# Sixteen pieces of like length: a recurrent chain dealt out anew between attention steps

## Chip, core and metric

The kernel runs on one core of a Trainium2 chip. The metric is the device time of one launch in microseconds, taken as the median of the runs.

## What is computed

One training step of a gated mix of two sequence layers on 2,048 tokens of width 576, with all gradients. Cut to the forward pass:

```
g   = sigmoid((x * gate_w).sum(-1))
a   = A(x)      # attention, 32 heads of 18; one k and one v head for all of them
b   = B(x)      # 64 segments of 32 tokens, 32 heads of 128, one after the other:
      h   = [mem (8 rows), segment (32 rows)]
      q, k, v = h Wq, h Wk, h Wv                 # masked softmax attention in h
      o   = softmax(q k^T * scale + mask) v Wo
      mem = o[:8]; the segment's output is o[8:]
out = g * a + (1 - g) * b
```

The outputs are `out` and the gradients of a scalar product with `grad_out`, for the input and every weight. Inputs and outputs are bf16.

## The kernel before

**Stages.** The program is a row of stages. First come weights and transposes, and projections of the tokens. Then comes the stage that the change is about, the forward weave. After it come all of layer B's token rows in bulk, a second weave (the chain backward with pass 2 of attention A), and the weight gradients.

**The weave.** `weave` takes two Python generators and alternates between them: one piece of the chain, then one step of the sweep, with the order of instructions on each engine just as written (`manual_schedule`). The chain is `b_chain_fwd`: layer B's eight memory rows through 64 segments, 16 pieces to a segment. The sweep is `a_pass1`: 1,024 steps, 16 for each block of one head pair and 512 queries. So piece i of a segment always stands before step i of a block.

**A step.** Step n issues on PE the scores matmuls `a_S` of step n+1 (two tiles of 32 rows), the matmuls `a_dP` of step n, the products with `a_W` of step n-1, and the products with `a_E` of step n, both into `a_acc`. ACT takes the exp of the scores (line 1401, 128x1024), DVE multiplies `a_dP` by `a_E` into `a_W` (line 1434, two instructions). `a_S` has one buffer of two PSUM banks, `a_dP` three of one bank, `a_acc` one. At the end of a block, in its step 16, ACT copies `a_acc` into `a_acs` (line 1439). The first product of the next block waits for that copy, and it is issued in step 1.

**Post-processing of a block.** `a_post` has three parts, which the sweep calls at the end of steps 1, 4 and 6 of the next block. The first transposes `a_acs` in f32 on PE, and ACT copies the result to `a_tk` (line 1472). The second transposes `a_QD`, and ACT copies it to `a_qt` (line 1478, one buffer). The third is one reciprocal on DVE, eleven small operations on POOL, and three stores on SP: `otok`, `dqtok` (lines 1498, 1504) and `sd` from `a_qt` (line 1508). The parts use the chain's PSUM tile `c_pj`.

**A piece.** The chain's projections are [40 rows of memory and riding tokens] x 576 x 4,096 for each of k, q and v, in two halves j. A half is 20 matmuls: five k-tiles of 128 rows, each with four matmuls of 512 columns on the four column tiles of the array. It accumulates in one PSUM bank, and ACT moves it to SBUF (`evac`, line 63). The pieces of a segment before:

| piece | work on PE |
|---|---|
| 0, 1 | k projection, half 0, half 1 |
| 2 | transpose of k (`mem_T`, 8 matmuls with full-width weights) |
| 3, 4 | q projection |
| 5 | transpose of q |
| 6 | v projection, half 0 |
| 7 | scores of 32 heads, 65 small matmuls (`ps`), then exp |
| 8 | denominator (2 matmuls), then reciprocal on DVE |
| 9 | v projection, half 1 |
| 10 | transpose of v |
| 11 | product with v (`po`, 16 matmuls) |
| 12, 13, 14 | output projection in thirds of 256, 256 and 64 columns (32 matmuls each); sums over head groups of the third before (f32 matmuls) |
| 15 | last sum; DVE copies the new memory into `hm` (line 419) |

The projections, the v transpose and the thirds use the PSUM tile `c_pj`, the others `c_x`; each is one bank with one buffer.

**Riding tokens and transfers.** Beside the memory rows, `hm` carries up to 24 tokens whose q, k and v are wanted later in the chain. SP loads them a segment ahead (line 254). In the first 48 segments SP also transposes the weight heads, two a segment, into the one buffer `c_wt` (line 275), and stores each again (line 279, `stash_end`). SP further copies rows between DRAM buffers (lines 303, 305), loads `c_kx` (line 262), `c_vx` (line 268) and `a_QD` (line 1390), and writes `oh`. Transfers of POOL carry the projected rows out. All of SP's transfers go out in the order written.

Of the kernel before, what the change touches and what calls it, by code (L numbers as in the profile page):

```python
# [10 lines left out]
F32 = mybir.dt.float32  # L11
P = 128

D = 576
NKT = 5
# [15 lines left out]
class Kern:  # L31
# [205 lines left out]
    def b_chain_fwd(self, keep, sp, psum):  # L237
        nc = self.nc
        NSEG = self.NSEG
# [3 lines left out]
        for kt in range(NKT):  # L243
            rows = KT_ROWS[kt]
            nc.gpsimd.dma_start(hm[0][0:rows, kt, 0:8], self.B_mem0[:, kt * P:kt * P + rows].rearrange("m d -> d m"))

        def ride(s):
            t0 = self.XT0 * P + 24 * s
            return t0, max(0, min(24, self.T - t0))

        def load_ride(s):
            t0, n = ride(s)
            if n:
                nc.sync.dma_start(hm[s % 2][:, :, 8:8 + n], self.xT_dram[:, :, t0:t0 + n].rearrange("k p t -> p k t"))
# [23 lines left out]
        def stash_end(t, c):  # L278
            nc.sync.dma_start(self.st_WT[c // HB][:, c % HB, :], t[:])
# [3 lines left out]
        def flat(t, j):  # L283
            return t[:, 4 * j:4 * j + 4, :].rearrange("p u e -> p (u e)")

        kx, vx = load_k(0), load_v(0)
        for s in range(NSEG):
            h_ = hm[s % 2]
            nc.gpsimd.dma_start(self.memT_dram[:, :, s, :], h_[:, :, 0:8])
            t2 = {w: sp.tile([P, 8, E], BF16, name=f"c_{w}2", bufs=1) for w in ("k", "q", "v")}  # L290
            mT = {w: sp.tile([P, 4, 8, 8], BF16, name=f"c_{w}mT", bufs=2) for w in ("k", "v")}

            def head_out():
                c0 = 8 * (s % 16)
                nc.sync.dma_start(self.oh_dram[s // 16][:, :, c0:c0 + 8], oh[:].rearrange("p c u q -> p (c u) q"))

            def rows_out(w):
                nc.gpsimd.dma_start(self.row_dram[w][s], t2[w][:].rearrange("p u e -> p (u e)"))

            def rows_copy(w):  # L300
                src = self.row_dram[w][s].rearrange("(c r) e -> c r e", r=32)
                t0, n = ride(s)
                nc.sync.dma_start(self.mtok[w][s * 8:(s + 1) * 8, :].rearrange("r (c e) -> c r e", c=4), src[:, 0:8, :])
                if n:
                    nc.sync.dma_start(self.xtok[w][t0:t0 + n, :].rearrange("r (c e) -> c r e", c=4), src[:, 8:8 + n, :])

            def mT_out(w, src):
                nc.scalar.copy(mT[w][:].rearrange("p c u t -> p u c t"), src)
                nc.gpsimd.dma_start(self.mTd[w][s], mT[w][:].rearrange("p c u t -> p (c u) t"))

            def proj(w, j):
                pj = self.proj_mem(h_, self.W[w], j, psum, "c_pj", 1)
                self.evac(flat(t2[w], j), pj[:], use="s")

            if 0 < s <= 48:
                stash_end(*wt)
            for j in range(2):
                proj("k", j)
                if j == 0:
                    if s + 1 < NSEG:  # L320
                        load_ride(s + 1)
                    nc.gpsimd.dma_start(self.pq_dram[s // 4].rearrange("s q c w k -> (s q c) w k")
                                        [:, 4 * (s % 4):4 * (s % 4) + 4, :], self.zeros[:].unsqueeze(1).to_broadcast([P, 4, P]))
                yield
            src = self.mem_T(t2["k"], psum, "c_x", 1)
            mT_out("k", src)
            rows_out("k")
            yield
            for j in range(2):
                proj("q", j)  # L330
                yield
            src = self.mem_T(t2["q"], psum, "c_x", 1)
            qT = sp.tile([P, 8, 4, 8], BF16, name="c_qT", bufs=1)
            nc.vector.tensor_copy(qT[:], src)
            rows_out("q")
            yield
            rows_copy("k")
            proj("v", 0)
            if s < 48:
                wt = stash(2 * s)  # L340
            yield
            ps = psum.tile([P, P], F32, name="c_x", bufs=1)
            self.mm(ps[:], lhsT=self.identB[:], rhs=self.mbias[:], start=True, stop=False)
            for u in range(8):
                for c in range(4):
# [6 lines left out]
            Et = sp.tile([P, 2, 64], BF16, name="c_E", bufs=1)  # L352
            nc.scalar.activation(Et[:].rearrange("p a b -> p (a b)"), ps[:], ACT.Exp, scale=SCALEB)
            yield
            den = psum.tile([P, 64], F32, name="c_x", bufs=1)
            self.mm(den[:], lhsT=self.blockones[:], rhs=Et[:, 0, :], start=True, stop=False)
            self.mm(den[:], lhsT=self.blockones[:], rhs=Et[:, 1, :], start=False, stop=True)
            rd = sp.tile([P, 64], F32, name="c_rd", bufs=1)
            nc.vector.reciprocal(rd[:], den[:])
            yield  # L360
            proj("v", 1)
            if s + 1 < NSEG:
                kx = load_k(s + 1)
            pn = sp.tile([P, 2, 64], BF16, name="c_pn", bufs=1)
# [4 lines left out]
            rows_out("v")  # L369
            yield  # L370
            rows_copy("q")
            src = self.mem_T(t2["v"], psum, "c_pj", 1)
            mT_out("v", src)
            yield
            po = psum.tile([P, 8, 32], F32, name="c_x", bufs=1)
# [10 lines left out]
            if s + 1 < NSEG:  # L386
                vx = load_v(s + 1)

                def half(lo, hi):
                    ph = psum.tile([P, 512], F32, name="c_pj", bufs=1)  # L390
                    for u in range(8):
                        for g in range(4):
                            self.mm(ph[32 * g:32 * g + 32, 0:hi - lo], lhsT=oT[:, u].rearrange("p c q -> p (c q)"),
                                    rhs=self.WoN[:, 8 * g + u, lo:hi], start=(u == 0), stop=(u == 7), tp=(0, 32 * g))
                    return ph

                def sums(hs, kts):
                    for n, kt in enumerate(kts):
                        ncols = KT_ROWS[kt]
                        self.mm(pm[0:ncols, kt, :], lhsT=hs[:, n * P:n * P + ncols], rhs=self.selF[:, :])  # L400

                head_out()
                rows_copy("v")
                if s < 48:
                    stash_end(*wt)
                    wt = stash(2 * s + 1)
                hn = hm[(s + 1) % 2]
                hs = None
                pm = None
                for lo, hi in ((0, 256), (256, 512), (512, 576), (576, 576)):  # L410
                    if hi > lo:
                        ph = half(lo, hi)
                    if lo:
                        kts = range(lo // P - 2, min(lo // P, NKT)) if lo < 576 else (4,)
                        if pm is None:
                            pm = psum.tile([P, NKT, 8], F32, name="c_x", bufs=1)
                        sums(hs, kts)
                        r = 64 if lo == 576 else P
                        nc.vector.tensor_copy(hn[0:r, kts[0]:kts[-1] + 1, 0:8], pm[0:r, kts[0]:kts[-1] + 1, :])
                    if hi > lo:  # L420
                        hs = sp.tile([P, 256], F32, name="c_hs", bufs=1)
                        nc.scalar.copy(hs[:, 0:hi - lo], ph[:, 0:hi - lo])
                    yield
            else:
                yield
                head_out()
                rows_copy("v")
                yield
# [950 lines left out]
    def a_pass1(self, keep, sp, psum, xps):  # L1379
        nc = self.nc  # L1380
# [34 lines left out]
        post = None  # L1415
        for n in range(NP_ + 1):
            if n < NP_:
                kt = n % 16
                if kt == 8:
                    load(n // 16 + 2)  # L1420
                if n > 1 and n % 16 == 1:
                    acc = psum.tile([P, 512], F32, name="a_acc", bufs=1)
                    acc_mm(acc, n - 1, E_, self.VK, True, False)
                if n + 1 < NP_:
                    mm_S(n + 1)
                dP = [psum.tile([P, 512], F32, name="a_dP", bufs=3) for _ in range(2)]
                for i in range(2):
                    r = slice(64 + 32 * i, 96 + 32 * i)
                    self.mm(dP[i][:], lhsT=self.KV[r, kt * P:kt * P + P], rhs=QD[n // 16][r, :], tp=(64 + 32 * i, 0))
                if n + 1 < NP_:  # L1430
                    ex(n + 1)
                W_[n] = sp.tile([P, 2, 512], BF16, name="a_W", bufs=2)
                for i in range(2):
                    nc.vector.tensor_tensor(out=W_[n][:, i, :], in0=dP[i][:], in1=E_[n][:, i, :], op=ALU.mult)  # L1434
            if n > 0:
                acc_mm(acc, n - 1, W_, self.WK, False, n % 16 == 0)
                if n % 16 == 0:
                    acs = sp.tile([P, 512], F32, name="a_acs", bufs=1)
                    nc.scalar.copy(acs[:], acc[:])
                    bb = n // 16 - 1  # L1440
                    post = self.a_post(bb // 4, bb % 4, acs, QD.pop(bb), sp, xps, dl_all)
            if n < NP_:
                if n == 0:
                    acc = psum.tile([P, 512], F32, name="a_acc", bufs=1)
                if n % 16 or n == 0:
                    acc_mm(acc, n, E_, self.VK, n == 0, False)
            if post is not None and n % 16 in (1, 4, 6):
                if next(post, "end") == "end":
                    post = None
            yield  # L1450
# [359 lines left out]
```

The softmax here doesn't subtract the row's maximum and nothing guards it: scores larger than these inputs give would overflow.

## Time and profile before

| | |
|---|---|
| three runs | 6,305.22, 6,307.33 and 6,308.78 us |
| profiled execution | span 6,318.6 us |
| PE busy in the span | 5,710.0 us, 90% |
| DVE, ACT, POOL busy | 59%, 55%, 31% |
| forward weave (first to last `a_S` matmul) | 507.7 to 2,393.2 us |
| TensorE clock granted, 1,000 to 1,200 us | 1.00 |

The profile records one execution, some 11 us longer than the runs. A matmul's row gives the time until its modelled end; the next one starts earlier, since matmuls are pipelined, so lengths of pieces are read from starts. In a line of the timeline the first number is the start in us, the second the length, then engine, line of code, operation and tiles; the brackets give idle time of the engine and what ended it. SP has rows only for what its queue issues.

### The profile page before, as it was taken

How to read it: one execution, taken by the hardware profiler on the slowest of the kernel's cores; microseconds unless marked ns; L12 is line 12 of the kernel's file. 1: busy time of each engine (PE TensorE's matmuls, PEld its weight loads, DVE VectorE, ACT ScalarE, POOL GpSimd, SP SyncE). 2: the span in 40 equal slices, each digit the busy share in tenths (PEclk: the TensorE clock that was granted, in tenths of full speed). 3: DMA queues.
4: the chain of work that ended last, by engine and by line, in shares of the span. 5: the costliest groups of instructions: out<-in, count | busy, mean ns of one | idle time of the engine just before them, and what ended most of it. 6: DMA issues, size and time to landing. Idle time of an engine off the chain costs nothing.

```text
span 6318.6 us, 209026 instructions
## 1 busy us (share of the span) xinstructions
PE 5710.0 (90%) x88822; PEld 3385.4 (54%) x88822; DVE 3755.0 (59%) x7061; ACT 3486.0 (55%) x5105; POOL 1956.0 (31%) x3451
## 2 busy tenths in 40 slices
PE   7898999999999994999969999999998999899996
PEld 5443444444444443877735555555554777674443
DVE  4335777777777773666658888888887111121111
ACT  3326777777777773665647777777776222111101
POOL 3002333333333333444423333333333111122212
PEclk9999999999999997999989999999999999999998
DMA  4636778777776544999974444444443999986643
GB/s 152 226 151 113 117 119 124 120 121 123 119 124 112 99 86 140 256 253 257 254 228 106 108 110 110 111 106 107 108 109 101 246 236 240 246 259 204 220 148 113
DMA packets 1368110, 991.96 MB, mean 157 GB/s; under 512 B 931613, under 2 KB 1184806, under 8 KB 1356486
## 3 DMA queue, kind: packets, MB, share of 16 engines
q1 hardware_dynamic: 1285030, 780.53, 52.4%
q0 software_dynamic: 82144, 198.05, 10.9%
q8 instruction: 696, 11.40, 0.8%
q14 instruction: 240, 1.97, 0.1%
HBM read 552.41 MB, written 384.76 MB: 148 GB/s over the span
## 4 chain that ended last, share of the span: by engine, by line
PE 64%; ACT 18%; issue 8%; DMA 6%; SPq 2%; POOL 1%; DVE 1%; ACTq 0%; POOLq 0%; DVEq 0%
ACT b_E L1543 10%; PE w_acc L66 10%; PE c_pj L66 7%; PE a_acc L66 6%; PE b_S L66 6%; ACT a_E L1401 5%; PE a_S L66 5%; PE p_pb L66 4%; PE r_pj L66 4%; DMA dsx_dram<-x_dS 3%; PE r_x L66 2%; PE x_tr L71 2%; PE b_acc L66 2%; PE c_x L66 2%; PE y_pdx L66 2%
## 5 line engine op out<-in xcount | busy, mean ns | idle before, releaser
L1434 DVE TENSOR_TENSOR a_W<-a_dP,a_E 128x512 bf16<-128x512 f32 x2048 | 1315.5, 684 | 430.5 <-PE a_dP L66 368.2
L1564 DVE TENSOR_TENSOR b_dS<-b_dP,b_E 128x512 bf16<-128x512 f32 x2048 | 1313.2, 683 | 239.6 <-issue 119.9
L1543 ACT ACTIVATE b_E<-b_S 128x1024 bf16<-128x1024 f32 x1024 | 1048.9, 1024 | 444.3 <-PE b_dP L66 320.8
L1401 ACT ACTIVATE a_E<-a_S 128x1024 bf16<-128x1024 f32 x1024 | 1051.6, 1027 | 159.0 <-PE a_dP L66 141.7
L66 PE MATMUL b_S<-b_KV,b_QD 32*128 32x512 bf16 x2048 | 400.3, 381 | 155.8 <-ACT b_E L1543 101.3
L66 PE MATMUL r_pj<-WT,r_dT 128*32 128x288 bf16 x12288 | 493.3, 287 | 1.1 <-DMA WT<-st_WT 1.1
L66 PE MATMUL a_S<-a_QD,l_KV 32*128 32x512 bf16 x2048 | 399.1, 383 | 104.1 <-ACT a_E L1401 95.3
L66 PE MATMUL w_acc<-w_d,w_h 128*128 128x512 bf16 (+1 forms) x2400 | 473.8, 379 | 0.0
L66 PE MATMUL b_acc<-b_dS,b_SD 128*32 128x512 bf16 x2048 | 419.3, 390 | 0.4 <-DVE b_dS L1564 0.2
L66 PE MATMUL a_acc<-a_W,l_WK 128*32 128x512 bf16 x4096 | 413.8, 390 | 1.1 <-issue 0.9
L66 PE MATMUL a_acc<-a_E,l_VK 128*32 128x512 bf16 x4096 | 404.3, 380 | 10.9 <-issue 1.9
L66 PE MATMUL b_acc<-b_E,b_SD 128*32 128x512 bf16 x2048 | 403.4, 390 | 0.0
L66 PE MATMUL b_dP<-b_KV,b_QD 32*128 32x512 bf16 x2048 | 399.9, 386 | 0.0
L66 PE MATMUL a_dP<-a_QD,l_KV 32*128 32x512 bf16 x2048 | 398.7, 385 | 0.5 <-issue 0.5
L66 PEld LDWEIGHTS <-r_dT 128*32 128x32 bf16 x12288 | 333.1, 97 | 80.0 <-issue 2.2
L1034 DVE COPY y_T<-y_pt 128x512 bf16<-128x512 bf16 x256 | 97.0, 420 | 467.3 <-PE y_pt L71 449.4
L66 PEld LDWEIGHTS <-b_QD 32*128 32x128 bf16 x4096 | 164.5, 91 | 346.4 <-issue 284.9
L66 PEld LDWEIGHTS <-w_h 128*128 128x128 bf16 (+1 forms) x2400 | 212.9, 100 | 244.7 <-issue 3.4
L66 PEld LDWEIGHTS <-hm 128*32 128x32 bf16 x7680 | 222.1, 97 | 219.8 <-issue 37.0
L66 PEld LDWEIGHTS <-l_KV 32*128 32x128 bf16 x4096 | 135.1, 91 | 284.1 <-issue 259.7
L1020 ACT CAST y_tdk<-y_pk 128x512 bf16<-128x512 f32 x128 | 75.1, 587 | 379.8 <-PE y_pk L66 216.7
L66 PE MATMUL y_pdx<-WT,y_T 128*128 128x288 bf16 x2048 | 273.3, 287 | 0.0
(410 smaller groups left out, 11437.3 us busy)
## 6 DMA issues: line engine op xcount, KB each, us to landing
b_QD<-qd_dram SPq DMA_DIRECT2D x256, 128.0 KB
b_SD<-sd_dram SPq DMA_DIRECT2D x256, 128.0 KB
dOx_dram<-p_tok SPq DMA_DIRECT2D x16, 1024.0 KB
c_vx<-vx_dram SPq DMA_DIRECT2D x256, 64.0 KB
krow_dram<-c_k POOLq DMA_DIRECT2D x64, 256.0 KB, 5.7
qrow_dram<-c_q POOLq DMA_DIRECT2D x64, 256.0 KB, 5.0
vrow_dram<-c_v POOLq DMA_DIRECT2D x64, 256.0 KB, 3.8
x_q<-qx_dram SPq DMA_DIRECT2D x32, 512.0 KB
```

The source lines that it names most:

```text
L66: return self.nc.tensor.matmul(out, lhsT, rhs, start=start, stop=stop, tile_position=tp, skip_group_check=True)
L71: return self.nc.tensor.transpose(out, in_, self.identB[b:b + nrows, b:b + nrows], tile_position=tp)
L1020: nc.scalar.copy(d[w][:, r, :], pk[:])
L1034: nc.vector.tensor_copy(T_[t][w][:], pt[:])
L1401: nc.scalar.activation(E_[n][:], S.pop(n)[:], ACT.Exp, scale=SCALEA)
L1434: nc.vector.tensor_tensor(out=W_[n][:, i, :], in0=dP[i][:], in1=E_[n][:, i, :], op=ALU.mult)
L1543: nc.scalar.activation(E_[n][:], S.pop(n)[:], ACT.Exp, scale=SCALEA)
L1564: nc.vector.tensor_tensor(out=D_[n][:, i, :], in0=dP[i][:], in1=E_[n][:, i, :], op=ALU.mult)
```

## The change

The pieces stay 16 to a segment, and each matmul is kept. What moves:

- The projections are cut at k-tiles, four matmuls each: k into 2 (in the last piece of the segment before), 3+1, 4; q into 2, 3+1, 4; v into 2, 3, then 3, 2. The parts stand in pieces 15, 0, 1, then 2 to 4, then 5, 6, 8 and 9.
- The halves use the tiles `c_x` and `c_pj` in turn, and so do the scores, the denominator, the transposes, the thirds of the output projection and the sums.
- The sums of the first third stand ahead of the last third in piece 14, those of the second and the last third in piece 15, with the copies into `hm`. `c_hs` has two buffers instead of one.
- The parts of `a_post` are called in steps 9, 10 and 12, and SP's load of `a_QD` in step 11 instead of 8.

The core of it:

```diff
-            for j in range(2):
-                proj("k", j)
...
+            if s == 0:
+                proj("k", 0, (0, 1), "c_x")
+            else:
+                pj["k", 0] = k0
+            proj("k", 0, (2, 3, 4), "c_x")
+            proj("k", 1, (0,), "c_pj")
...
+            yield
+            proj("k", 1, (1, 2, 3, 4), "c_pj")
+            yield
             src = self.mem_T(t2["k"], psum, "c_x", 1)
             mT_out("k", src)
             rows_out("k")
-            yield
-            for j in range(2):
-                proj("q", j)
-                yield
-            src = self.mem_T(t2["q"], psum, "c_x", 1)
+            proj("q", 0, (0, 1), "c_pj")
+            yield
+            proj("q", 0, (2, 3, 4), "c_pj")
+            proj("q", 1, (0,), "c_x")
+            yield
+            proj("q", 1, (1, 2, 3, 4), "c_x")
+            yield
+            src = self.mem_T(t2["q"], psum, "c_pj", 1)
...
+            proj("v", 0, (0, 1), "c_x")
             yield
             rows_copy("k")
-            proj("v", 0)
+            proj("v", 0, (2, 3, 4), "c_x")
...
+            proj("v", 1, (0, 1, 2), "c_x")
+            den = psum.tile([P, 64], F32, name="c_pj", bufs=1)
...
-            proj("v", 1)
+            proj("v", 1, (3, 4), "c_x")
...
+                hs0 = half(0, 256, "c_pj")
+                yield
+                hs1 = half(256, 512, "c_x")
+                yield
+                pm = psum.tile([P, NKT, 8], F32, name="c_pj", bufs=1)
+                sums(hs0, (0, 1))
+                copies(0, 2)
+                hs2 = half(512, 576, "c_x")
+                yield
+                sums(hs1, (2, 3))
+                sums(hs2, (4,))
+                del pj["k", 0]
+                proj("k", 0, (0, 1), "c_x", hn)
+                k0 = pj["k", 0]
+                copies(2, 4)
+                copies(4, 5, 64)
+                yield
...
-                if kt == 8:
+                if kt == 11:
                     load(n // 16 + 2)
...
-            if post is not None and n % 16 in (1, 4, 6):
+            if post is not None and n % 16 in (9, 10, 12):
```

More of the change, by code (lines that the diff above doesn't have):

```diff
@@ L309, in mT_out, with proj @@
                 nc.gpsimd.dma_start(self.mTd[w][s], mT[w][:].rearrange("p c u t -> p (c u) t"))
-            def proj(w, j):
-                pj = self.proj_mem(h_, self.W[w], j, psum, "c_pj", 1)
-                self.evac(flat(t2[w], j), pj[:], use="s")
+            pj = {}
+            def proj(w, j, kts, name, h=None):
+                if (w, j) not in pj:
+                    pj[w, j] = psum.tile([P, 512], F32, name=name, bufs=1)
+                self.proj_part(pj[w, j], h_ if h is None else h, self.W[w], j, kts)
+                if kts[-1] == NKT - 1:
+                    self.evac(flat(t2[w], j), pj[w, j][:], use="s")
             if 0 < s <= 48:
                 stash_end(*wt)
-            for j in range(2):
-                proj("k", j)
[L319 to L323, printed above, removed]
-                yield
+            if s == 0:
[4 more added lines that the diff above has]
+            proj("k", 1, (0,), "c_pj")
+            if s + 1 < NSEG:
+                load_ride(s + 1)
+            nc.gpsimd.dma_start(self.pq_dram[s // 4].rearrange("s q c w k -> (s q c) w k")
+                                [:, 4 * (s % 4):4 * (s % 4) + 4, :], self.zeros[:].unsqueeze(1).to_broadcast([P, 4, P]))
+            yield
+            proj("k", 1, (1, 2, 3, 4), "c_pj")
+            yield
             src = self.mem_T(t2["k"], psum, "c_x", 1)
@@ L341, in b_chain_fwd @@
             yield
-            ps = psum.tile([P, P], F32, name="c_x", bufs=1)
+            ps = psum.tile([P, P], F32, name="c_pj", bufs=1)
             self.mm(ps[:], lhsT=self.identB[:], rhs=self.mbias[:], start=True, stop=False)
@@ L354, in b_chain_fwd @@
             yield
-            den = psum.tile([P, 64], F32, name="c_x", bufs=1)
+            proj("v", 1, (0, 1, 2), "c_x")
+            den = psum.tile([P, 64], F32, name="c_pj", bufs=1)
             self.mm(den[:], lhsT=self.blockones[:], rhs=Et[:, 0, :], start=True, stop=False)
@@ L371, in b_chain_fwd @@
             rows_copy("q")
-            src = self.mem_T(t2["v"], psum, "c_pj", 1)
+            src = self.mem_T(t2["v"], psum, "c_x", 1)
             mT_out("v", src)
@@ L387, in b_chain_fwd, with half @@
                 vx = load_v(s + 1)
-                def half(lo, hi):
-                    ph = psum.tile([P, 512], F32, name="c_pj", bufs=1)
+                def half(lo, hi, name):
+                    ph = psum.tile([P, 512], F32, name=name, bufs=1)
                     for u in range(8):
@@ L394, in half @@
                                     rhs=self.WoN[:, 8 * g + u, lo:hi], start=(u == 0), stop=(u == 7), tp=(0, 32 * g))
-                    return ph
+                    hs = sp.tile([P, 256], F32, name="c_hs", bufs=2)
+                    nc.scalar.copy(hs[:, 0:hi - lo], ph[:, 0:hi - lo])
+                    return hs
                 def sums(hs, kts):
@@ L400, in sums, with copies @@
                         self.mm(pm[0:ncols, kt, :], lhsT=hs[:, n * P:n * P + ncols], rhs=self.selF[:, :])
+                def copies(lo, hi, rows=P):
+                    nc.vector.tensor_copy(hn[0:rows, lo:hi, 0:8], pm[0:rows, lo:hi, :])
                 head_out()
@@ L407, in b_chain_fwd @@
                 hn = hm[(s + 1) % 2]
[L408 to L423, printed above, removed]
+                hs0 = half(0, 256, "c_pj")
[15 more added lines that the diff above has]
+                yield
             else:
```

## The prediction

> **What bounds the kernel now.** I looked first for the stretch that the change touches. The tile view of a_S, the attention scores of pass 1, has its first matmul at 507.7 us and its last at 2393.2: 1,024 weave steps in 1,885.5 us, 1.843 us each, 29.49 us for a segment of 16. The stage view of one stretch inside it reads
>
> ```profile
> 1000.00:1200.00 200.00, 188.42 (x3620) 94.27 (x3616) 152.64 (x274) 153.73 (x213) 74.12 (x148) 1.00 0.79 121
> ```
>
> (PE, PEld, DVE, ACT, POOL busy, TensorE clock, DMA share, GB/s). PE is busy 94%, ACT and DVE 77%: PE's order sets the pace, but not everywhere. The timeline shows where it does not:
>
> ```profile
> 1204.46 0.39 PE L66 MATMUL a_S<-a_QD,l_KV 32*128 32x512 bf16 x2 [0.52 <-ACT a_E L1401]
> 1204.94 1.02 ACT L1401 ACTIVATE a_E<-a_S 128x1024 bf16<-128x1024 f32 x1 [0.53 <-PE a_dP L66]
> 1205.23 1.25 PE L66 MATMUL c_pj<-Wv,hm 128*32 128x512 bf16 x20
> 1206.42 0.39 PE L66 MATMUL a_S<-a_QD,l_KV 32*128 32x512 bf16 x2
> 1206.54 0.59 ACT L63 CAST c_v<-c_pj 128x512 bf16<-128x512 f32 x1 [0.57 <-PE c_pj L66]
> 1207.02 1.03 ACT L1401 ACTIVATE a_E<-a_S 128x1024 bf16<-128x1024 f32 x1
> 1208.10 0.39 PE L66 MATMUL a_S<-a_QD,l_KV 32*128 32x512 bf16 x2 [0.44 <-ACT a_E L1401]
> ```
>
> I call interval i the time from the a_S matmul before piece i to the one behind it. Interval 9 (the second v projection) runs 1204.46 to 1206.42, 1.96 us, and PE never waits. Interval 10, a short piece, lasts 1.68: a_S has one buffer, so it waits for the exp, which itself started late behind the evacuation c_v. The 16 intervals of this segment (1187.49 to 1216.85) are 1.99, 2.48, 1.65, 1.95, 1.95, 1.69, 1.95, 1.68, 1.63, 1.96, 1.68, 1.55, 1.75, 2.29, 1.65, 1.51, sum 29.36; the two segments before it lasted 29.28 each (k projection at 1129.70, 1158.98, 1188.26). So heavy pieces are PE's and light ones the exp loop's: start 0.48 us after a_S, 1.02 long, 0.05 to the next a_S, 1.55 in all. Interval 1 is special:
>
> ```profile
> 1220.34 0.59 ACT L1439 COPY a_acs<-a_acc 128x512 f32<-128x512 f32 x1
> 1220.98 0.40 PE L66 MATMUL a_acc<-a_E,l_VK 128*32 128x512 bf16 x4
> 1221.32 0.39 PE L66 MATMUL a_S<-a_QD,l_KV 32*128 32x512 bf16 x2
> ```
>
> Here PE waits for the accumulator's copy. Last, SP's queue, for 48 of the 64 segments:
>
> ```profile
> 1229.24 1.15 SPq L279 DMA_DIRECT2D st_WT<-c_wt  x1
> 1236.93 1.18 SPq L275 DMA_TRANSPOSE c_wt<-in_B_Wk_dram  x1
> 1239.64 0.37 SPq L279 DMA_DIRECT2D st_WT<-c_wt  x1
> 1240.06 0.45 SPq L254 DMA_DIRECT2D hm<-xT_dram  x1
> 1242.08 1.49 SPq L275 DMA_TRANSPOSE c_wt<-in_B_Wk_dram  x1
> 1244.79 0.50 SPq L1508 DMA_DIRECT2D sd_dram<-a_qt  x1
> ```
>
> SP stands 6.5 us between the first two (one c_wt buffer, its store must land) and 1.5 us before the third; otherwise it issues without pause. It runs 10 to 26 us behind the pieces and needs 28 to 31 us a segment (hm is issued at 1179.66, 1209.28, 1240.06, 1268.30), as much as PE. Nobody waits for it yet.
>
> **What the skill says.** "TensorE: Matmul & The Clock Gate", section "Wait — 56ns, not 53.3ns?": warm matmuls start N/2.4 + 2.5 ns apart, 216 ns for 512 columns. Twenty matmuls on four column tiles should take 5 x 0.216 = 1.08 us; the trace has 1.19 from 1205.23 to 1206.42, so 0.11 of tail. "TensorEngine Tiling (Array Packing)", "Key Properties": changing the tiling mode drains the array. The trace agrees: full-width weights begin 0.87 us after a_S (1207.29), 32-column weights' matmuls 0.77. "PSUM — Partial Sum Buffer", "Terms": two engines must not touch one bank and quadrant at once, so one bank means that a projection waits for the evacuation. In the segment read above PE never stands for that reason, so the second bank earns nothing itself; it permits the split.
>
> **The change part by part.** No matmul is added or removed. Per interval, n groups of four projection matmuls cost 0.77 + 0.216 n + 0.11: 1.74 at four groups, 1.53 at three, 1.31 at two.
> - Intervals 0, 3, 4: five groups become four, 1.74 each (1.99, 1.95, 1.95): -0.67.
> - Interval 1: the k evacuation begins before a_S, so the exp starts at 0.48 instead of 0.59; then 0.91 to the copy, 0.64 to the accumulation, 0.34 to a_S: 2.37 (2.48), -0.11.
> - Intervals 2 and 5: a transpose (0.87 + 0.30) and two groups, 0.43 + 0.11: 1.71 (1.65, 1.69): +0.08.
> - Interval 6: three groups, 1.53; the exp loop's 1.55 rules (1.95): -0.40. Interval 7 stays at 1.68.
> - Interval 8: three groups and the denominator, about 0.25: 1.77 (1.63; 1.55 in the shorter segments): +0.14. Its reciprocal, 0.55, still ends before the next a_W may begin.
> - Interval 9: two groups, 1.31; exp loop 1.55 (1.96): -0.41.
> - Interval 10: the post-processing's f32 transposes come here instead of interval 2, beside the same kind of transpose: 1.65 (1.68), -0.03.
> - Interval 11: its bf16 transposes beside po: PE 1.69. But the copies a_tk and c_vmT stand ahead of the exp, which starts 0.71 late, as at 1223.68 after 1222.97: 0.71 + 1.02 + 0.05 = 1.78 (1.55), +0.23.
> - Interval 12 stays. Interval 13 loses the f32 sums, 0.54: 1.75 (2.29), -0.54.
> - Interval 14: sums ahead of the short third: 0.87 + 0.54 + 0.35 + 0.07 = 1.83, bounds 1.65 (as now) and 1.87; I take 1.80: +0.15.
> - Interval 15: three sums, 0.74, and two groups: 0.87 + 0.74 + 0.43 + 0.11 = 2.15 (1.51), +0.64. The copies into hn end while PE is in the step's own 0.77.
>
> The sum is -0.92 against 29.36, so 28.44; against the commoner 29.28 it is -0.84. Bounds: each mixed interval (2, 5, 8, 14, 15) may miss by 0.1, together 0.4 to 1.3 gained.
>
> SP: the load of a_QD moves three steps later, behind the k transpose and the q copies; it fetches for a block five steps further on, so it hides. The three stores of the post-processing (otok, dqtok, sd) move from step 6, ahead of c_kx, to step 12, behind the second c_wt transpose. That fills the 1.5 us stand there, but their packets now precede the store that the next c_wt waits for. No row shows that landing delay: below it is nothing (SP then needs about 27.8, today's 29.4 less 1.6), above it is the 6.5 us of the other stand. The three stores are small beside what precedes that stand, so I take 1 us: 28.8 at worst, about PE's new pace. I charge 0.15 us a segment for it, 7 us. Behind the stores wait the ride load of hm, now needed one piece sooner, and a_qt, with one buffer: the ACT copy of step 10 cannot start before sd has landed. POOL's eleven small operations move too, to pieces 13 to 15, where POOL stands.
>
> 64 x 0.84 = 54, less 7: 47 us. The profiled span is 6,318.6, so its like would be 6,272; the runs, 6,307.33, become 6,260. Later stages only begin earlier.
>
> **The rivals.** (a) SP becomes the bound while the weights are transposed. For it: it is as long as PE now. If it needs 29.2, those 48 segments gain 0.2, the last 16 0.84: 23 us, 6,284. Against it: one stand is filled. (b) Slower: the landing of sd. Today the second c_wt transpose is issued 26 us after its piece (1236.93 against 1210.4); sd would follow it and land some 7 us after the a_qt copy's turn at 1238. ACT then stands, and with it exp and PE, until SP's own period is the stage's. It decides from about 29.7 us of SP's period; if the landing takes 3.5 us instead of 1, the period is 31.3, and 48 x 1.8 = 86 less 13 gives 6,380; at 30.2, 6,330. Against it: SP's lag shrinks with the filled stand. (c) More: mixed pieces overlap better and stalls of the instruction stream shrink: 1.3 x 64 = 83, 6,224. (d) The pieces are evened but DVE or the exp loop takes all back: 6,300 to 6,314.
>
> **How the numbers follow.** Measurement tells 0.2%, 12.6 us, from no change. Main forecast 0.57, 6,232 to 6,278; (a) 0.16; (c) 0.08; (d) 0.07; (b) 0.12. Faster 0.81, same 0.07, slower 0.12. The range 6,220 to 6,302 takes in the main case, (a), most of (c) and part of (d).
>
> **What would show it.** Intervals 3, 4, 13 at 1.74 to 1.75, 6 and 9 at 1.55, 15 near 2.15, spacing of k projections near 28.4. Wrong if ACT's a_qt copy waits for the sd store, if PE waits for hm, if interval 15 exceeds 2.4, or if intervals 8 to 11 show PE waiting for a_W.

## The result and the profile after

The changed kernel took 6,248.23 us (median of four runs, 6,245.49 to 6,254.85), the kernel before 6,306.27 us beside it: 0.991 of the time, 95% interval 0.9893 to 0.9927, 58 us less. The prediction was 6,260.

The profiled span is 6,243.7 us, 74.9 less than the one before. The weave accounts for 71.0: its first `a_S` matmul stands at 507.4, its last at 2,321.9, 1,814.5 us in place of 1,885.5. The stage view of the changed kernel, in the same stretch as in the prediction (PE, PEld, DVE, ACT, POOL busy, clock, DMA share, GB/s):

```profile
1000.00:1200.00 200.00, 194.59 (x3756) 89.83 (x3749) 156.49 (x283) 159.98 (x220) 75.37 (x154) 1.00 0.68 126
```

PE is busy 97% instead of 94%, at the same clock, and does 3,756 matmuls in the time of 3,620. A matmul is busy as long as before on average (0.052 us in both); less time is left between.

The intervals tell where. Interval i runs from the `a_S` matmul ahead of piece i to the one behind it; these are the medians over the segments after the first, in us, read from the starts of `a_S` in the trace:

```
interval          0    1    2    3    4    5    6    7    8    9   10   11   12   13   14   15    sum
before          1.99 2.48 1.65 1.95 1.95 1.68 1.95 1.68 1.55 1.95 1.68 1.55 1.75 2.29 1.66 1.50  29.28
predicted       1.74 2.37 1.71 1.74 1.74 1.71 1.55 1.68 1.77 1.55 1.65 1.78 1.75 1.75 1.80 2.15  28.44
after           1.74 2.36 1.72 1.74 1.74 1.72 1.55 1.65 1.69 1.55 1.65 1.81 1.75 1.75 1.76 2.17  28.34
```

The timeline of the changed kernel shows a lightened piece at the exp loop's floor. It is interval 9, with two groups of four matmuls where five stood:

```profile
1177.36 0.39 PE L66 MATMUL a_S<-a_QD,l_KV 32*128 32x512 bf16 x2
1177.84 1.02 ACT L1422 ACTIVATE a_E<-a_S 128x1024 bf16<-128x1024 f32 x1 [0.66 <-PE a_dP L66]
1178.12 0.61 PE L66 MATMUL c_x<-Wv,hm 128*32 128x512 bf16 x8
1178.78 0.59 ACT L63 CAST c_v<-c_x 128x512 bf16<-128x512 f32 x1
1178.91 0.39 PE L66 MATMUL a_S<-a_QD,l_KV 32*128 32x512 bf16 x2 [0.18 <-ACT a_E L1422]
1179.39 1.02 ACT L1422 ACTIVATE a_E<-a_S 128x1024 bf16<-128x1024 f32 x1
```

The evacuation `c_v` (line 63) no longer stands ahead of the exp: it begins before `a_S`, and the next exp starts 0.48 us after its scores (1179.39 - 1178.91), not 0.60.

Interval 1, the longest, still waits for the copy of the accumulator:

```profile
1163.57 1.02 ACT L1422 ACTIVATE a_E<-a_S 128x1024 bf16<-128x1024 f32 x1
1164.49 0.58 ACT L1460 COPY a_acs<-a_acc 128x512 f32<-128x512 f32 x1
1165.12 0.40 PE L66 MATMUL a_acc<-a_E,l_VK 128*32 128x512 bf16 x4 [0.44 <-ACT a_acs L1460]
1165.46 0.39 PE L66 MATMUL a_S<-a_QD,l_KV 32*128 32x512 bf16 x2
```

And SP, whose queue I had feared, as its timeline in the changed kernel shows it (lines left out are marked):

```profile
1165.95 1.17 SPq L275 DMA_TRANSPOSE c_wt<-in_B_Wk_dram  x1
1167.23 0.52 SPq L1519 DMA_DIRECT2D otok_dram<-a_ot  x1
1167.84 0.46 SPq L1525 DMA_DIRECT2D dqtok_dram<-a_dq  x1
1168.38 0.46 SPq L1529 DMA_DIRECT2D sd_dram<-a_qt  x1
1168.94 0.38 SPq L279 DMA_DIRECT2D st_WT<-c_wt  x1
1169.37 0.60 SPq L254 DMA_DIRECT2D hm<-xT_dram  x1
...
1177.59 0.56 SPq L305 DMA_DIRECT2D qx_dram<-qrow_dram  x1
1181.87 0.34 SPq L1411 DMA_DIRECT2D a_QD<-qd_dram  x1
```

The stand of 1.5 us between a transpose and its store is filled by the three stores, as foreseen. But between `qx` and `a_QD` SP now waits 3.7 us. The load takes the buffer that the post-processing's transposes read last, now in step 10 and before in step 4; SP has caught up with PE, which only then gives the buffer back. The waits of SP's queue between 600 and 1,880 us (total, times, longest) put a number on it:

```profile
SPq L1411 <- PE c_x L66: 177.0, 45, 4.4
```

In the kernel before, the same load (line 1390) has only 12 us of such waits:

```profile
SPq L1390 <- PE a_dP L66: 7.2, 15, 1.3
SPq L1390 <- PE c_x L66: 4.8, 9, 0.9
```

### The profile page after: what moved, and what is told of

It reads as the page before. It is cut to its first block, busy times and chain, and to the rows that moved or that the text cites. A ratio compares the mean times of both kernels' runs of the same rounds, so it can differ in the third digit from the quotient of the medians.

```text
span 6243.7 us, 208736 instructions
## 1 busy us (share of the span) xinstructions
PE 5691.9 (91%) x88611; PEld 3321.0 (53%) x88822; DVE 3743.0 (60%) x7061; ACT 3500.1 (56%) x5105; POOL 1952.9 (31%) x3451
## 4 chain that ended last, share of the span: by engine, by line
PE 64%; ACT 15%; issue 9%; DMA 6%; SPq 3%; POOL 2%; DVE 1%; ACTq 0%; POOLq 0%; DVEq 0%
ACT b_E L1564 10%; PE w_acc L66 10%; PE a_acc L66 8%; PE c_x L66 6%; PE b_S L66 6%; PE a_S L66 5%; PE c_pj L66 5%; PE p_pb L66 4%; PE r_pj L66 4%; ACT a_E L1422 3%; PE r_x L66 2%; DMA dsx_dram<-x_dS 2%; PE x_tr L71 2%; PE b_acc L66 2%; PE x_po L66 1%
## 5 line engine op out<-in xcount | busy, mean ns | idle before, releaser
L66 PEld LDWEIGHTS <-hm 128*32 128x32 bf16 x7680 | 188.2, 96 | 186.4 <-issue 14.6
L66 PEld LDWEIGHTS <-l_KV 32*128 32x128 bf16 x4096 | 118.9, 91 | 297.4 <-issue 275.3
```

Of the source, the lines that this page charges most:

```text
L66: return self.nc.tensor.matmul(out, lhsT, rhs, start=start, stop=stop, tile_position=tp, skip_group_check=True)
```

## The experiments

All ratios are to the kernel before, measured beside each set. Its median was 6,304.2 us beside the post-processing moved alone and moved back, the one bank and the first run with k whole; 6,305.4 beside the thirds, k later, the accumulator's product and "Both"; 6,301.5 beside the load alone, the v copy and "All three". The result above has 6,306.27, so a difference to the changed kernel, 6,248.23, is uncertain by up to 5 us from the sets alone. The medians of the intervals, where a kernel's differ from those of the kernel it was made from, stand with each run.

**The post-processing moved alone.** The question was whether SP's relief is the gain.

```diff
 (the kernel before)
-                if kt == 8:
+                if kt == 11:
...
-            if post is not None and n % 16 in (1, 4, 6):
+            if post is not None and n % 16 in (9, 10, 12):
...
-            src = self.mem_T(t2["v"], psum, "c_pj", 1)
+            src = self.mem_T(t2["v"], psum, "c_x", 1)
```

> The kernel before with one part of the change alone: the post-processing in steps 9, 10, 12 and the a_QD load in step 11 (the v transpose takes the bank c_x, so that it need not wait for the copy a_tk). The theory of the intervals: interval 2 loses the f32 transposes and falls to the exp loop's 1.55 (from 1.65), interval 11 rises to 1.78 (from 1.55), 5 and 10 stay at 1.68: +0.13 us a segment, about 8 us slower than before, 6,314. The rival, that the gain came from SP's queue being relieved: this kernel then has most of the gain, 6,250 to 6,270. On SP itself I expect the second stand (1.65 us) to go; if it is the order of the stores that took the lag away in the changed kernel, SP waits for PE before a_QD here too; if it was the finer pieces, SP stays behind by 10 to 20 us.

Measured: 6,316.13 us, ratio 1.002 (1.0014 to 1.0027). Interval 2 fell to 1.55, interval 11 rose to 1.78, the rest stayed: 29.41 against 29.28, the +0.13 expected. SP was relieved here too:

```profile
SPq L1390 <- PE c_x L66: 188.0, 43, 4.8
```

So SP's relief came without any gain, and the move by itself costs some 12 us, of which the medians of the intervals show 8. SP was not the bound in the kernel before.

**Only the load moved.** The question was which part of the move relieved SP.

```diff
 (the kernel before)
-                if kt == 8:
+                if kt == 11:
```

> The kernel before with only the a_QD load moved from step 8 to step 11; the three stores of the post-processing stay in step 6. On the time: no change, 6,305. On SP: if the place of the three stores is what relieved its queue, it still waits 6.5 us and 1.5 us for c_wt, and for PE before a_QD at most little; if the load's place did it, SP waits some 4 us a segment for PE before a_QD, as in the changed kernel.

Measured: 6,298.27 us, ratio 0.9992 (0.9984 to 1.0001), intervals unchanged to 0.01. SP's longer waits have none for PE before `a_QD`, but these:

```profile
SPq L275 <- DMA st_WT<-c_wt: 283.2, 54, 7.1
SPq L1498 <- POOL a_t L1500: 85.2, 39, 3.4
SPq L1504 <- POOL a_dq L1503: 40.4, 41, 1.0
SPq L1508 <- POOL a_qt L1505: 27.1, 43, 0.7
```

The run cannot tell what it was meant to tell. With the transposes still in step 4, the buffer is free long before step 11, so no wait for PE can show up at the load, however little SP lags. And SP had caught up here too: it waits some 3.5 us a segment for POOL's results ahead of the three stores, for which the profile before has 15 us in all. The run with the thirds alone, below, issues SP's transfers in the very order of the kernel before, and waits for POOL as well, 131 us in all; the largest part:

```profile
SPq L1501 <- POOL a_t L1503: 63.0, 34, 2.8
```

The lag of the `hm` load says the same. Taken from the `a_S` ahead of the piece in which it is written to its issue, the median over segments 4 to 47 is 20.9 us in the profile before, 12.8 with the thirds alone, 12.4 with only the load moved, 8.4 with the post-processing moved alone and 8.6 in the changed kernel. So some 4 us of lag go with the place of the stores. The other 8 are gone in the run with SP's old order too; of the kernel before there is one profile, and whether the larger lag belongs to the kernel or to that one execution is not shown.

**The post-processing moved back.** The question was whether the cut pieces need it elsewhere.

```diff
 (the changed kernel)
-                if kt == 11:
+                if kt == 8:
...
-            if post is not None and n % 16 in (9, 10, 12):
+            if post is not None and n % 16 in (1, 4, 6):
```

> The changed kernel with the post-processing back in steps 1, 4, 6 and the load in step 8. It takes its bank c_pj, which the cut projections now hold at that point. The theory of the intervals with the bank as a resource: in interval 2 the q matmuls wait for the copy a_tk (ends 2.2 us after a_S), 2.8 in place of 1.72; in interval 5 the q transpose waits for the copy a_qt, 3.0 in place of 1.72; intervals 10 and 11 fall to 1.55: +2.05 us a segment, about 130 us slower than the changed kernel, 6,379. The rival, that the place of the post-processing matters only for ACT and PE time: -0.1 us a segment and no wait for a_tk or a_qt, 6,240.

Measured: 6,372.83 us, ratio 1.0107 (1.0092 to 1.0123). Interval 2 is 2.80, interval 5 2.99, intervals 10 and 11 are 1.55; the sum is 30.34, 2.00 more than in the changed kernel. The timeline shows the bank handed over:

```profile
1184.16 0.58 ACT L1493 COPY a_tk<-c_pj 128x512 f32<-128x512 f32 x1
1184.79 0.61 PE L66 MATMUL c_pj<-Wq,hm 128*32 128x512 bf16 x8 [0.54 <-ACT a_tk L1493]
```

PE's q matmuls start as the copy ends. So the move, which costs 12 us alone, is what makes the cuts possible: with the cuts, its absence costs 125.

**One bank for q.**

```diff
 (the changed kernel)
-            proj("q", 1, (0,), "c_x")
+            proj("q", 1, (0,), "c_pj")
             yield
-            proj("q", 1, (1, 2, 3, 4), "c_x")
+            proj("q", 1, (1, 2, 3, 4), "c_pj")
```

> The changed kernel with both q halves in the one bank c_pj instead of two in turn. If the second bank is what permits the cut 3+1, the first four matmuls of the second half wait in piece 3 for ACT's evacuation of the first (start 0.23 after its last matmul, 0.59 long): interval 3 becomes about 2.6 in place of 1.74, 64 x 0.85 = 55 us slower than the changed kernel, 6,303: the cut's gain is gone. If the bank plays no part, 6,248.

Measured: 6,307.09 us, ratio 1.0006 (0.9998 to 1.0014). Only interval 3 changed, from 1.74 to 2.61. Among PE's waits (600 to 2,350 us) stands, once a segment, what the changed kernel has not:

```profile
PE c_pj L66 <- ACT c_q L63: 41.3, 60, 0.7
```

The timeline has the wait between the two parts of piece 3:

```profile
1194.20 0.82 PE L66 MATMUL c_pj<-Wq,hm 128*32 128x512 bf16 x12
1195.07 0.58 ACT L63 CAST c_q<-c_pj 128x512 bf16<-128x512 f32 x1
1195.71 0.40 PE L66 MATMUL c_pj<-Wq,hm 128*32 128x512 bf16 x4 [0.69 <-ACT c_q L63]
```

One projection on one bank eats the whole gain of the change, 59 us. A piece with parts of two halves needs the second bank.

**The thirds alone.** The output projection's two banks, `c_hs` with two buffers, and the sums one piece later, on the kernel before; the k projection as before.

```diff
 (the kernel before; the loop over thirds becomes)
+                hs0 = half(0, 256, "c_pj")
+                yield
+                hs1 = half(256, 512, "c_x")
+                yield
+                pm = psum.tile([P, NKT, 8], F32, name="c_pj", bufs=1)
+                sums(hs0, (0, 1))
+                copies(0, 2)
+                hs2 = half(512, 576, "c_x")
+                yield
+                sums(hs1, (2, 3))
+                sums(hs2, (4,))
+                copies(2, 4)
+                copies(4, 5, 64)
+                yield
```

> The kernel before with another part of the change alone: the thirds of the output projection in two banks, c_hs with two buffers, the sums one piece later. Theory of the intervals: 13 falls from 2.29 to 1.75, 14 rises from 1.66 to 1.76, 15 from 1.51 to 1.63 (as in the run with the whole k projection), 0 falls by 0.04: -0.36 us a segment, 23 us faster than before, 6,282. The rival, that only pieces evened all through pay, because the exp loop gives short intervals nothing back: no gain, 6,304.

Measured: 6,285.3 us, ratio 0.9968 (0.9955 to 0.998), 20 us less. Intervals 13, 14, 15: 1.75, 1.76, 1.63; interval 0 1.95, interval 1 2.49; sum 28.94, 0.34 less than before. An interval that was under-filled (15, at 1.50 by the exp loop) took 0.5 us of PE work for 0.13 of time: the gain needs only one long and one short interval, not evenness all through.

**k whole again.** The part of the change that begins the next k projection in piece 15, undone.

```diff
 (the changed kernel)
-            proj("k", 0, (2, 3, 4), "c_x")
-            proj("k", 1, (0,), "c_pj")
+            proj("k", 0, range(NKT), "c_x")
...
-            proj("k", 1, (1, 2, 3, 4), "c_pj")
+            proj("k", 1, range(NKT), "c_pj")
...
-                proj("k", 0, (0, 1), "c_x", hn)
```

> The changed kernel with the k projection whole again, half 0 in piece 0 and half 1 in piece 1, nothing of it in the segment before. Interval 1 is set by ACT's copy of the accumulator (2.36), in which PE has room for one more group of four matmuls. Theory of the intervals: interval 15 1.74 (from 2.17), interval 0 1.96 to 2.0 (from 1.74), interval 1 still 2.36: -0.2 us a segment, 13 us faster than the changed kernel, 6,235: beginning k early then costs time. The rival, that the early start hides the wait for the new memory: interval 0 then has a wait for hm of 0.3 or more, and the kernel is not faster than 6,248.

Measured: 6,231.15 us, ratio 0.9883 (0.987 to 0.9897): 17 us faster than the changed kernel. Intervals 15, 0, 1: 1.63, 1.95, 2.49 against 2.17, 1.74, 2.36, together 0.20 less, as expected, though not as I split it: interval 1 rose by 0.13, because the evacuation of the first half stands ahead of the exp again and the copy behind it, and interval 15 fell by 0.54, not 0.43. No wait for `hm` appeared. The intervals give 13 us of the 17, and against its own measurement of the kernel before the run gains 15 more than the changed kernel. Beginning k early costs time.

**k later.** If PE has room in interval 1, k belongs there.

```diff
 (the changed kernel)
-            proj("k", 0, (2, 3, 4), "c_x")
-            proj("k", 1, (0,), "c_pj")
+            proj("k", 0, (0, 1, 2, 3), "c_x")
...
-            proj("k", 1, (1, 2, 3, 4), "c_pj")
+            proj("k", 0, (4,), "c_x")
+            proj("k", 1, range(NKT), "c_pj")
...
-                proj("k", 0, (0, 1), "c_x", hn)
```

> The changed kernel with the k projection moved later, not earlier: four groups of half 0 in piece 0, its last group and the whole of half 1 in piece 1, none in piece 15. Interval 15 1.63, interval 0 1.74, interval 1 still 2.36, set by the copy a_acs, since no evacuation stands before its exp; interval 2 1.72: -0.54 us a segment against the changed kernel, 35 us, 6,213. The rival: six groups fill PE in interval 1, or two evacuations in a row delay the exp of interval 2, and it is no better than the whole k projection, 6,231.

Measured: 6,209.23 us, ratio 0.9853 (0.984 to 0.9867). Intervals 0, 1, 2, 15: 1.74, 2.36, 1.72, 1.63. Two more groups, eight matmuls, went into interval 1 without lengthening it: they lie in PE's wait for `a_acs`, which the changed kernel has once a segment (26.0 us in 59 waits, shown below) and this run no longer has.

**The accumulator's first product behind the scores.** The other way to use that wait is not to let `a_S` stand behind it.

```diff
 (the changed kernel; a_pass1)
-                if n > 1 and n % 16 == 1:
-                    acc = psum.tile([P, 512], F32, name="a_acc", bufs=1)
-                    acc_mm(acc, n - 1, E_, self.VK, True, False)
                 if n + 1 < NP_:
                     mm_S(n + 1)
                 dP = [psum.tile([P, 512], F32, name="a_dP", bufs=3) for _ in range(2)]
...
+                if n > 1 and n % 16 == 1:
+                    acc = psum.tile([P, 512], F32, name="a_acc", bufs=1)
+                    acc_mm(acc, n - 1, E_, self.VK, True, False)
                 if n + 1 < NP_:
                     ex(n + 1)
```

> The changed kernel with the first product of a block into a_acc issued after the scores and a_dP of step 1 instead of ahead of them. If interval 1 is set by ACT's copy a_acs, as I read it, a_S no longer waits for it: interval 1 falls from 2.36 to the exp loop's 1.55; PE's wait moves behind a_S and the exp of step 2 starts 0.9 late, so interval 2 rises from 1.72 to 2.09: -0.44 us a segment, 28 us faster than the changed kernel, 6,220. The rival, that the copy's wait only moves (all of it comes back in interval 2): 6,245 to 6,250.

Measured: 6,215.24 us, ratio 0.9861 (0.9846 to 0.9876). Intervals 1 and 2: 1.55 and 2.08. The wait does move, as the rival said, but interval 1 fell by 0.81 and interval 2 rose by only 0.36: the rest of it is covered by the scores, `a_dP` and the exp.

**Both.** k whole, as above, and the first product behind the scores.

> A candidate for a better version: k projection whole in pieces 0 and 1, and the first product of a block after the scores. Intervals 15, 0, 1, 2: 1.63, 1.95, 1.74, 2.0 against 2.17, 1.74, 2.36, 1.72 of the changed kernel: -0.67 us a segment, 43 us, 6,205. If the two do not add, because the wait for the copy only moves into interval 2: 6,230.

Measured: 6,203.73 us, ratio 0.9843 (0.9829 to 0.9856). Intervals 15, 0, 1, 2: 1.63, 1.95, 1.74, 2.03; sum 27.70, 0.64 less than in the changed kernel.

**The v copy on DVE.** Interval 11 is the one that the moved post-processing lengthened. In the changed kernel its exp stands behind two copies:

```profile
1180.53 0.59 ACT L1493 COPY a_tk<-c_pj 128x512 f32<-128x512 f32 x1
1180.57 0.39 PE L66 MATMUL a_S<-a_QD,l_KV 32*128 32x512 bf16 x2
...
1181.02 0.38 ACT L308 CAST c_vmT<-c_x 128x256 bf16<-128x256 f32 x1
...
1181.28 1.04 ACT L1422 ACTIVATE a_E<-a_S 128x1024 bf16<-128x1024 f32 x1
...
1182.37 0.39 PE L66 MATMUL a_S<-a_QD,l_KV 32*128 32x512 bf16 x2
```

```diff
 (the changed kernel; mT_out)
-                nc.scalar.copy(mT[w][:].rearrange("p c u t -> p u c t"), src)
+                (nc.vector.tensor_copy if w == "v" else nc.scalar.copy)(mT[w][:].rearrange("p c u t -> p u c t"), src)
```

> The changed kernel with the copy of the transposed v on DVE instead of ACT. If interval 11 is set by the exp that stands behind the two copies a_tk and c_vmT on ACT (0.71 late), it falls from 1.81 to PE's 1.69: 64 x 0.12 = 8 us faster than the changed kernel, 6,240. The rival, that DVE then delays a_W in interval 11 or 12 and PE waits for it: 6,248 or more.

Measured: 6,234.61 us, ratio 0.9888 (0.9871 to 0.9904). Interval 11 fell to 1.59, not 1.69:

```profile
1176.42 0.39 PE L66 MATMUL a_S<-a_QD,l_KV 32*128 32x512 bf16 x2
1176.53 0.42 DVE L308 CAST c_vmT<-c_x 128x256 bf16<-128x256 f32 x1
1176.90 1.02 ACT L1422 ACTIVATE a_E<-a_S 128x1024 bf16<-128x1024 f32 x1
...
1178.02 0.39 PE L66 MATMUL a_S<-a_QD,l_KV 32*128 32x512 bf16 x2
```

The exp starts 0.48 after its scores. I had put PE's own work in interval 11 at 1.69; it is at most 1.59. The intervals give 14 us; the medians differ by 14, and by 9 if each is taken against its own measurement of the kernel before.

**All three.** k whole, first product behind the scores, v copy on DVE.

> The last candidate: k projection whole, first product of a block behind the scores, copy of the transposed v on DVE. If the three add: 6,203.7 less 8 us, 6,196. If DVE takes the last part back: 6,204.

Measured: 6,188.63 us, ratio 0.9817 (0.9802 to 0.9831), sum of the intervals 27.49. This version beats both kernels, the changed one by 60 us (55 if each is taken against its own measurement of the kernel before; the intervals, 0.85 less, give 54), with the change's cuts of q and v, its banks and its thirds, and without its early k.

## Why the prediction was right

**The pace.** The forecast was a sum over 16 intervals, PE's work in the heavy ones and the exp loop or ACT's copies in the others. Each of the 16 came within 0.04 but for interval 8, and undoing or moving single parts changed the intervals that the sum names. None of the signs of being wrong appeared. Interval 15 stayed under 2.4, and PE's waits in the changed kernel (600 to 2,300 us) are these two:

```profile
PE a_acc L66 <- ACT a_acs L1460: 26.0, 59, 0.4
PE a_S L66 <- ACT a_E L1422: 11.3, 61, 0.3
```

**Single terms.** Whole groups removed (0, 3, 4, 6, 9): exact to 0.01. Interval 1, by ACT's chain: 2.37 against 2.36. Mixed pieces 2 and 5: 1.71 against 1.72. Interval 11 by the two copies: 1.78 against 1.81, and the run with the copy on DVE shows that it was ACT. Intervals 14 and 15: 1.80 and 2.15 against 1.76 and 2.17. The one term that missed was interval 8, "about 0.25" for the denominator: interval 8 came to 1.69, not 1.77, so 0.17 by the same sum. PE's denominator matmuls run from 1177.19 to `a_S` at 1177.36.

**The charge for SP.** This was the weak step. I let the moved stores cost 0.15 us a segment, 7 us, a figure that no sum of the prediction gives: its own worst case, 28.8, is 0.36 above 28.44. Neither rival that rests on SP came near. No row of the changed kernel has ACT waiting for `sd`, or PE for the load of the riding tokens, and SP waited for PE before `a_QD` 3.9 us a segment (177.0 in 45 waits). Its lag of 10 to 26 us was no proof that it was full; I had read its pace, equal to PE's, as its limit. Without this charge the forecast would have been 54 us; 58 was measured.

**A reading that was off.** The prediction says that in the segment read PE never stands for a bank. In interval 1 it did:

```profile
1189.48 0.39 PE L66 MATMUL a_S<-a_QD,l_KV 32*128 32x512 bf16 x2
1189.59 0.59 ACT L63 CAST c_k<-c_pj 128x512 bf16<-128x512 f32 x1 [0.60 <-PE c_pj L66]
1190.22 1.26 PE L66 MATMUL c_pj<-Wk,hm 128*32 128x512 bf16 x20
```

The second half of k begins as the copy of the first ends, 0.74 us after `a_S`. In the run with k whole on two banks it begins 0.55 after (1161.01 and 1161.56). That the second bank earns nothing there still holds, 2.48 against 2.49, because the copy of the accumulator ends later.

**Profile and runs.** The profiled spans differ by 75 us, the runs by 58. The medians of the intervals give 64 x 0.94 = 60. The rest of the profile's difference is single long intervals in the execution before: there the means of the intervals add to 29.48 against medians of 29.28 (12 us over 60-odd segments), here 28.37 against 28.34. That execution took 6,320.41 us, 13 more than the median of the runs.

**What the prediction did not see.** It priced the early k at +0.64 in interval 15 and its gains in intervals 0 and 1, and did not ask what the cheapest place for those groups was. The rows for it were there: interval 1, with its wait for `a_acs`, had room.

**What stays open.** Why SP lagged so much more in the profile before than in every other run, those with its order of transfers included. Its issues took longer there (the `vm` store, line 303, 4.28 us in the segment shown before and 2.19 in the changed kernel); which transfers collided was not tried. The cuts of q and v were not run alone either: they need the move of the post-processing and the second bank, as two runs show, so their share of the gain is only read from the intervals: 2 to 10, where they stand, are together 1.03 shorter, the moved post-processing included.

## What to carry to other kernels

In a weave whose order is fixed, lay out each interval as the larger of two sums, the busy engine's work in it and the loop of the other engine, and move work from intervals of the first kind to those of the second; the sums can be read from start-to-start times of one profile and held here to 0.04 us in 15 of 16 intervals. Look first for an interval in which the busy engine itself waits: eight matmuls put there were free, and eight put too early cost some 15 us. Before cutting work across pieces, list who holds each PSUM bank at every cut, since a single bank handed over late costs 0.87 us, nearly all of the 0.94 that the whole change gains.

## What the runs showed of the hardware that I had not expected

- A wait of PE for a PSUM bank that ACT evacuates costs half as much again as the copy. In the run with one bank for q the interval grew by 0.87 us: 0.58 for the copy (1195.07), 0.06 from its end to the next matmul (1195.71), and 0.22 before it. In the run with the post-processing moved back, 0.05 lay between copy and matmul (1184.74 and 1184.79).
- ACT's rows overlap: an exp of 1.02 us is followed 0.92 us after its start by the copy `a_acs` (1163.57, 1164.49). The Trainium skill, "ScalarE: Activation LUTs", section "What ACT_TABLE_LOAD costs", says that back-to-back ACTIVATEs overlap by about 93 ns; the trace agrees with 0.10. So adding up the lengths of ACT's rows overstates the time they take here.
- A DMA queue that runs 10 to 26 us behind its program need not be full. With the same order of transfers, in the run with the thirds alone, SP found 131 us in which to wait for POOL; with the three stores moved it waited some 4 us a segment for PE. Neither the kernel with the load moved (0.9992) nor the one with the post-processing moved (1.002) gained from it.
